# Another order inside the dense unit of a fused Fourier filter and tanh-shrink layer: second layer as 3, 3, 5, 3 calls, transform steps behind the copies out of bank X

## Chip, cores, metric

One core of one Trainium2 chip. The metric is device time of the whole program in microseconds (us).

## The reference

```python
X = np.fft.rfft(x, axis=1)                       # x: 8 x 3008 x 256, fp32
y = np.fft.irfft(X * (filt_r + 1j * filt_i), n=3008, axis=1)
h = y.reshape(24064, 256) @ w_in                 # 256 x 2048
out = (h - np.tanh(h)) @ w_out                   # 2048 x 256
```

## The kernel before

The sequences are transformed in five batches. While one batch goes through the two matrix layers, the next is transformed in between, a step at a time. Both layers use a seven-product scheme for 2 x 2 blocks: seven products q = 1 to 7 and some adds in place of eight products.

The dense work runs in 192 **units**. In unit U, `up` makes the seven first-layer products, `shrink` works on the activation of unit U-1, and `down` makes the second-layer products of unit U-2. Four units make a group; their second layer accumulates in four PSUM banks (o0 to o3), and is read out in the group's last unit (`done`). Three more banks, X, Y and Z, hold first-layer results, and one bank serves all transform steps. That makes eight banks in all. The transform's matmuls write pf (first stage), pz and pe (middle stage, before and after the filter) and pu (last stage); zs is ScalarE's copy of pz, and uv is VectorE's product of pz with the filter.

```python
        # up(U, d, e, s, t): before
        mm(X, 1, True)
        mm(Y, 2, True)
        s1 = copied("s1")                 # ACT.copy out of X
        t(0)                              # transform step, if one is due here
        d()                               # a group of second-layer products
        s()                               # activation: arctan, square
        V.tensor_add(h[:, 0, :, 0:w], Y, s1)
        e()                               # in a group's last unit: read-out
        s()                               # activation: second square; VectorE multiply
        s()                               # VectorE multiply-add
        t(1)
        mm(X, 6, False)
        mm(Z, 5, True)
        u2 = copied("u2")                 # ACT.copy out of X
        d(); s(); e()
        t(2)
        mm(X, 7, False)
        u3 = copied("u3")                 # ACT.copy out of X
        V.tensor_add(h[:, 3, :, 0:w], Z, u3)
        d(); s(); e()
        t(3)
        mm(X, 4, False)
        V.tensor_copy(h[:, 2, :, 0:w], X) # VectorE copy out of X
        s(); d(); e()
        t(4)
        mm(Z, 3, False)
        V.tensor_add(h[:, 1, :, 0:w], Z, u2)
```

`mm(bank, q, ...)` is two **calls** (two halves of the hidden dimension); a call shows up as two MATMUL instructions. Bank X is one buffer: q6 accumulates onto q1 after s1 was copied out, q7 after u2, q4 after u3, and the next unit's q1 overwrites it after the VectorE copy.

```python
        # down(U): before (cut)
        at = {1: (0, 0), 2: (0, 1), 3: (1, 0), 5: (1, 1), 6: (2, 0), 7: (2, 1), 4: (3, 0)}  # q: (bank, half)
        mm(1, 2);  yield
        if done: ACT.copy(p1, product(1)); V.tensor_add(o[:, 0, 0:w], product(2), p1)
        yield
        mm(3, 5);  yield
        if done: ACT.copy(p5, product(5)); V.tensor_add(x12, product(3), p5)
        yield
        mm(6, 7);  yield
        if done: V.tensor_add(u2, product(6), p1); V.tensor_add(p1, product(7), u2)
        yield
        mm(4);     yield
        if done: ...                      # the rest of the read-out
        yield
```

## Time and profile before

| | before |
|---|---|
| time, median of 5 | 2882.08 us (2880.47 to 2883.72) |
| TensorE busy | 95% of the span |
| next busiest, VectorE / ScalarE / GpSimd | 69% / 65% / 61% |
| TensorE time lost in and between units (my sum) | 120 us of 180 us in all |

In an unbroken run of matmuls, the next one starts a fixed time after the last (0.215 us at 256 columns). Whatever a distance between two starts has above that is time lost (a stretch of matmuls at half pace counts too), and I book it under the product that comes after it. The profile's own table of waits shows less: a matmul is drawn some 0.38 us long, so a wait below 0.16 us doesn't appear, and a wait that falls on a weight load is listed under PEld.

In the lines of the profile, PE is TensorE, PEld its weight loads, DVE is VectorE, ACT ScalarE and POOL GpSimd. A line in order of time has start, duration, engine, line of the program, operation, output and inputs, and in brackets how long the engine was idle before it and what ended that.

### The profile page before, as it was taken

What the parts mean: (1) busy time and instruction counts of PE and PEld (TensorE: products, weight loads), DVE (VectorE), ACT (ScalarE), POOL (GpSimd) and SP (SyncE); (2) the same over time, 40 slices, a digit from 0 to 9 for tenths busy, and PEclk for the clock granted to TensorE, in tenths of its full rate; (3) what the DMA queues carried; (4) which work ended last, traced back from release to release, by engine and by line L of the source; (5) the groups of instructions that cost most, each with busy time, mean ns of one, the idle gap of its engine ahead of it and who ended that gap; (6) DMA issues with size and microseconds to landing.
All of it is one profiled execution on the core that took longest, in us unless ns stands there. A gap on an engine that the chain in (4) does not pass through costs nothing.

```text
span 2879.3 us, 36469 instructions
## 1 busy us (share of the span) xinstructions
PE 2748.1 (95%) x12474; PEld 2278.9 (79%) x12474; DVE 1989.3 (69%) x2214; ACT 1872.2 (65%) x2460; POOL 1743.4 (61%) x1382
## 2 busy tenths in 40 slices
PE   5789999999999999999999999999999999999996
PEld 3467777888878787888877888888888888888885
DVE  4675666766776677766677777766777777777765
ACT  3555666666767676666666676666666676666663
POOL 4345777544677767645576777655476666555544
PEclk7889999999999999999999999999999999999998
DMA  9644443232233332222323233112233222110100
GB/s 270 180 150 116 114 110 91 62 93 81 70 76 84 76 75 53 57 81 83 87 71 75 68 78 81 36 45 67 51 75 81 53 55 56 24 28 16 26 11 16
DMA packets 328061, 217.46 MB, mean 76 GB/s; under 512 B 229085, under 2 KB 280405, under 8 KB 327674
## 3 DMA queue, kind: packets, MB, share of 16 engines
q1 hardware_dynamic: 273176, 160.50, 23.6%
q10 hardware_dynamic: 52738, 51.33, 5.9%
q0 software_dynamic: 1952, 3.22, 0.5%
q8 instruction: 100, 1.64, 0.2%
q14 instruction: 95, 0.78, 0.1%
HBM read 138.81 MB, written 79.17 MB: 76 GB/s over the span
## 4 chain that ended last, share of the span: by engine, by line
PE 69%; DVE 9%; ACT 8%; POOL 5%; issue 4%; DMA 3%; SPq 1%; ACTq 0%; DVEq 0%; POOLq 0%
PE o L590 27%; PE x L483 18%; PE z L483 8%; PE y L483 5%; PE pe L364 3%; PE pu L447 3%; DVE h L544 3%; PE pz L383 3%; ACT y L539 2%; PE pf L304 2%; ACT y L540 1%; POOL t L465 1%; ACT u L489 1%; DVE uv L398 1%; DVE h L519 1%
## 5 line engine op out<-in xcount | busy, mean ns | idle before, releaser
L590 PE MATMUL o<-t,wd 128*128 128x256 f32 (+2 forms) x3072 | 777.9, 376 | 1.8 <-POOL t L464 1.3
L544 DVE TENSOR_TENSOR h<-h,y 128x1024 f32<-128x1024 f32 (+2 forms) x384 | 589.7, 1536 | 256.1 <-ACT y L540 255.9
L462 POOL TENSOR_TENSOR t<-h 128x512 f32<-128x512 f32 (+2 forms) x192 | 240.1, 1250 | 767.5 <-DVE h L548 582.3
L590 PEld LDWEIGHTS o<-t,wd 128*128 128x128 f32 x3072 | 582.0, 191 | 74.4 <-POOL t L464 1.9
L483 PE MATMUL x<-tu,wu 128*128 128x256 f32 (+2 forms) x2304 | 592.2, 380 | 16.5 <-ACT u L489 15.5
L590 PE MATMUL o<-h,wd 128*128 128x256 f32 (+2 forms) x2304 | 581.6, 375 | 0.2 <-DVE h L548 0.2
L548 DVE SCALAR_TENSOR_TENSOR h<-sq,h 128x1024 f32<-128x1024 f32 (+2 forms) x384 | 566.6, 1476 | 20.8 <-ACT y L539 0.5
L483 PEld LDWEIGHTS x<-tu,wu 128*128 128x128 f32 x2304 | 430.2, 191 | 157.2 <-issue 73.2
L590 PEld LDWEIGHTS o<-h,wd 128*128 128x128 f32 x2304 | 431.3, 190 | 70.8 <-issue 18.5
L545 ACT ACTIVATE sq<-y,near_b 128x1024 f32<-128x1024 f32 (+2 forms) x384 | 435.4, 1134 | 5.8 <-DVE h L548 1.1
L539 ACT ACTIVATE y<-h 128x1024 f32<-128x1024 f32 (+2 forms) x384 | 400.0, 1042 | 14.8 <-ACT e L367 6.8
L489 ACT COPY s<-x 128x512 f32<-128x512 f32 (+2 forms) x192 | 110.7, 577 | 458.2 <-PE x L483 449.6
L540 ACT ACTIVATE y<-y 128x1024 f32<-128x1024 f32 (+2 forms) x384 | 399.3, 1040 | 12.2
L465 POOL TENSOR_TENSOR t<-t,h 128x512 f32<-128x512 f32 (+2 forms) x192 | 306.7, 1597 | 0.0
L489 ACT COPY u<-x 128x512 f32<-128x512 f32 (+2 forms) x384 | 219.2, 571 | 73.0 <-PE x L483 35.5
L399 POOL TENSOR_TENSOR zs<-zs,ft 128x512 f32<-128x512 f32 x112 | 166.3, 1485 | 142.3 <-ACT zs L397 142.2
L463 POOL TENSOR_TENSOR t<-h,t 128x512 f32<-128x512 f32 (+2 forms) x192 | 241.6, 1258 | 15.0
L464 POOL TENSOR_TENSOR t<-h 128x512 f32<-128x512 f32 (+2 forms) x192 | 249.5, 1300 | 0.0
L400 POOL TENSOR_TENSOR uv<-uv,zs 128x512 f32<-128x512 f32 x112 | 211.3, 1887 | 16.0 <-DVE uv L398 7.8
L483 PE MATMUL x<-ut,wu 128*128 128x256 f32 (+2 forms) x768 | 200.0, 383 | 12.2 <-DVE h L519 10.7
L483 PE MATMUL z<-tu,wu 128*128 128x256 f32 (+2 forms) x768 | 195.4, 377 | 0.5 <-DVE h L525 0.5
L483 PE MATMUL z<-ut,wu 128*128 128x256 f32 (+2 forms) x768 | 194.8, 376 | 0.0
(113 smaller groups left out, 3236.6 us busy)
## 6 DMA issues: line engine op xcount, KB each, us to landing
a<-ct SPq DMA_DIRECT2D x64, 384.0 KB
ct<-e ACTq DMA_DIRECT2D x128, 192.0 KB
ft<-filt SPq DMA_DIRECT2D x96, 256.0 KB
out_dram<-ot SPq DMA_DIRECT2D x1408, 16.0 KB
ct<-a ACTq DMA_DIRECT2D x80, 256.0 KB
x_sb<-in_x_dram SPq DMA_DIRECT2D x69, 256.0 KB
e<-ct SPq DMA_DIRECT2D x33, 512.0 KB
fg<-fg SPq DMA_DIRECT2D x40, 392.0 KB
```

Source lines behind the costliest of these rows:

```text
L462: G.tensor_sub(t[0], b[0][1], b[0][0])
L463: G.tensor_sub(t[1], b[1][1], t[0])
L464: G.tensor_sub(t[2], b[1][1], b[0][1])
L465: G.tensor_sub(t[3], t[1], b[1][0])
L483: nc.tensor.matmul(bank[:, k], wu[:, q - 1, (2 * u + k) * 128:(2 * u + k + 1) * 128], rhs[q - 1], start=(first and k == 0), stop=True, ski ...
L489: ACT.copy(t, X)
L539: ACT.activation(y[k], ht[k], AF.Arctan, scale=S)
L540: ACT.activation(y[k], y[k], AF.Square)
L544: V.tensor_mul(ht[k], ht[k], y[k])
L545: ACT.activation(sq[k], y[k], AF.Square, bias=near_b, scale=A)
L548: V.scalar_tensor_tensor(out=ht[k], in0=sq[k], scalar=K, in1=ht[k], op0=ALU.add, op1=ALU.mult)
L590: nc.tensor.matmul(product(q), wd[:, q - 1, (2 * u + k) * 128: (2 * u + k + 1) * 128], rhs[q - 1][:, k], start=(u == 0 and k == 0 and q == ...
```

## The change

The intent is the same distance, five calls, between each two products that write X, and a ScalarE and VectorE queue in which the copies out of X stand ahead of the transform's work. Core of the diff:

```diff
         mm(X, 1, True)
+        s1 = copied("s1")
         mm(Y, 2, True)
-        s1 = copied("s1")
         t(0)
 ...
+        mm(X, 6, False)
+        u2 = copied("u2")
+        mm(Z, 5, True)
         t(1)
-        mm(X, 6, False)
-        mm(Z, 5, True)
-        u2 = copied("u2")
         d(); s(); e()
-        t(2)
         mm(X, 7, False)
         u3 = copied("u3")
         V.tensor_add(h[:, 3, :, 0:w], Z, u3)
+        t(2)
         d(); s(); e()
-        t(3)
         mm(X, 4, False)
         V.tensor_copy(h[:, 2, :, 0:w], X)
+        t(3)
 ...                                   # t(4) likewise behind mm(Z, 3) and its add
-        mm(1, 2)
+        mm((1, 0), (2, 0), (1, 1))                       # (q, half)
         yield
         if done:
             ACT.copy(p1, product(1))
+        yield
+        mm((2, 1), (3, 0), (3, 1))
+        yield
+        if done:
             V.tensor_add(o[:, 0, 0:w], product(2), p1)
         yield
-        mm(3, 5)
+        mm((5, 0), (6, 0), (5, 1), (6, 1), (7, 0))
         yield
         if done:
             ACT.copy(p5, product(5))
+            V.tensor_add(u2, product(6), p1)
             V.tensor_add(x12, product(3), p5)
-        yield
-        mm(6, 7)
+            G.tensor_add(o[:, 0, w:2 * w], u2, x12)
+        yield
+        mm((7, 1), (4, 0), (4, 1))
         yield
 ...
```

More of the change, by code (lines that the diff above doesn't have):

```diff
@@ L522, in up @@
         e()
-        t(4)
         mm(Z, 3, False)
         V.tensor_add(h[:, 1, :, 0:w], Z, u2)
+        t(4)
     def shrink(U):
@@ L587, in mm @@
         def mm(*qs):
-            for k in range(2):
-                for q in qs:
-                    nc.tensor.matmul(product(q), wd[:, q - 1, (2 * u + k) * 128:
-                                                    (2 * u + k + 1) * 128],
-                                     rhs[q - 1][:, k], start=(u == 0 and k == 0 and q == qs[0]),
-                                     stop=(u == 3 and k == 1), skip_group_check=True)
+            for q, k in qs:
+                nc.tensor.matmul(product(q), wd[:, q - 1, (2 * u + k) * 128:(2 * u + k + 1) * 128],
+                                 rhs[q - 1][:, k],
+                                 start=(u == 0 and k == 0 and at[q][1] == 0),
+                                 stop=(u == 3 and k == 1), skip_group_check=True)
         done = u == 3
@@ L609, in down @@
             ACT.copy(p5, product(5))
+            V.tensor_add(u2, product(6), p1)
             V.tensor_add(x12, product(3), p5)
+            G.tensor_add(o[:, 0, w:2 * w], u2, x12)
         yield
-        mm(6, 7)
+        mm((7, 1), (4, 0), (4, 1))
         yield
         if done:
-            V.tensor_add(u2, product(6), p1)
             V.tensor_add(p1, product(7), u2)
-        yield
-        mm(4)
-        yield
-        if done:
             V.tensor_add(o[:, 1, 0:w], product(4), p1)
-            G.tensor_add(o[:, 0, w:2 * w], u2, x12)
             G.tensor_add(o[:, 1, w:2 * w], p1, p5)
```

## The prediction

> **What bounds the kernel now.** I read the page first, then the table of stretches, then who PE waited for, then the order of work inside single units. A "unit" is one of 192 rounds that computes seven first-layer products (q 1, 2, 6, 5, 7, 4, 3 into the PSUM banks X, Y, X, Z, X, X, Z), seven second-layer products in four groups (d), and up to five transform steps t(0) to t(4).
>
> ```profile
> PE 2748.1 (95%) x12474; PEld 2278.9 (79%) x12474; DVE 1989.3 (69%) x2214; ACT 1872.2 (65%) x2460; POOL 1743.4 (61%) x1382
> ```
> TensorE is busy 95% and every other engine at most 69%. The work is the same after the change, so only TensorE's idle moments can move the time.
>
> ```profile
> 121.70:537.50 415.80, 377.98 (x1556) 290.40 (x1555) 266.82 (x315) 266.96 (x363) 262.95 (x202) 0.96 0.43 113
> ...
> 1215.00:1892.00 677.00, 671.83 (x3052) 554.83 (x3052) 476.56 (x513) 458.87 (x600) 433.46 (x328) 1.00 0.29 73
> ```
> Columns are span, then PE, PEld, DVE, ACT and POOL busy time. The first 24 units leave PE idle 38 us; a later stretch of 48 units leaves 5 us. A matmul of 256 columns is shown as about 380 ns, but in an unbroken run the next starts 0.215 us after it, so short waits hide in the shown durations. I therefore summed, from the starts of single matmuls in the trace, what each start-to-start distance exceeds its usual value by (0.215 us at 256 columns). That gives about 180 us lost: 60 before the first unit, 60 in units 0 to 23, 60 in units 24 to 191. By what stood after the wait in units 24 to 191: q1 of the next unit 26 us, q4 9 us, q7 5 us, q6 under 1 us; the rest is spread thinly. These four are the products that write bank X and wait for a copy out of it.
>
> ```profile
> PE x L483 <- ACT u L489: 15.5, 12, 3.8
> PE pe L364 <- DVE uv L398: 13.5, 18, 2.6
> PE x L483 <- DVE h L519: 10.7, 26, 0.9
> ```
> The waits of PE (total us, times, longest) name the same two culprits: ScalarE's copies u and VectorE's copy h out of X. One such wait, in the timeline at 1636 to 1641 us:
>
> ```profile
> 1636.37 1.02 PE L383 MATMUL pz<-a,fg 94*128 94x512 f32 x2
> 1637.23 1.03 PE L483 MATMUL x<-tu,wu 128*128 128x256 f32 x4
> 1638.09 0.58 ACT L397 COPY zs<-pz 64x512 f32<-64x512 f32 x1
> 1639.11 0.69 DVE L398 TENSOR_TENSOR uv<-pz,ft 128x512 f32<-128x512 f32 x1 [1.03 <-ACT zs L397]
> 1639.72 0.68 DVE L519 COPY h<-x 128x512 f32<-128x512 f32 x1
> 1640.45 1.13 PE L483 MATMUL x<-ut,wu 128*128 128x256 f32 x4 [0.47 <-DVE h L519]
> ```
> q4 (1637.23) is done near 1638.3, but the copy starts at 1639.72, behind the transform's multiply uv, which itself waited for ScalarE. PE then stalls. The change aims at this.
>
> **What the Trainium skill says.** "PSUM — Partial Sum Buffer", section "Engine vs sequencer instructions": ScalarE and VectorE queues are strict FIFO, and matmuls keep program order. The lines above agree: h waits 1.4 us behind uv though its data is there. The same page, section "PSUM bank collisions raise a hardware error", has accesses of two engines to one bank kept apart; uv starting only after ScalarE's zs (1.03 us of idling) agrees. "TensorE: Matmul & The Clock Gate", section "What's actually happening": after an idle window the array runs at half clock. The trace agrees: after q4's wait of 3.8 us at 186.3 us its four matmuls take 2.08 us in place of 1.03.
>
> **The change part by part.** In units of one call (two matmuls, 0.43 us), the calls between a writer of X and the next writer of X:
> - q1 to q6: 6 before, 5 after.
> - q6 to q7: 6, then 5.
> - q7 to q4: 4, then 5.
> - q4 to next q1: 4, then 5.
>
> The amount of work is unchanged: 14 + 14 calls. The transform step t(1) moves from before q6 to between q5 and d; t(2) from before q7 to after it; t(3) from before q4 to after it and after the h copy; t(4) behind q3. On ScalarE and VectorE their copies and multiplies now queue behind the copy out of X. t(0) stays in place.
>
> Gain at q1: 26 us. VectorE's copy no longer queues behind uv of t(3). 25 units have that step at t(3); 23 of them stall, 9 us together. In the other units (15 us of waits) the copy hangs on the chain q7, copy, VectorE, copy; between q7 and the next q1 there are now 14 calls instead of 12, 0.86 us more, and t(2) as well. The waits there average about 0.6 us. I take 24 us as gone.
>
> Gain at q4: 9 us. 7 us fall in units with the step pz or pe at t(2), whose ScalarE copies (two of 0.59, or 0.58 plus 0.32 of DMA issue) stood ahead of the copy u3. Now they stand behind it, and one call more covers it. I take 8 us as gone.
>
> Loss at q7, where I differ from the intent. The copy u2 is often not released by q6: ScalarE reaches it late. Unit 28, without any stall before:
>
> ```profile
> 592.21 1.03 PE L483 MATMUL x<-ut,wu 128*128 128x256 f32 x4
> 593.27 0.58 ACT L489 COPY s<-x 128x512 f32<-128x512 f32 x1 [2.87 <-PE x L483]
> 593.93 1.02 PE L304 MATMUL pf<-x_sb,wf_sb 128*128 128x512 f32 x2
> 594.99 0.58 ACT L305 COPY a<-pf 128x512 f32<-128x512 f32 x1 [1.14 <-PE pf L304]
> 595.61 0.37 ACTq L306 DMA_DIRECT2D ct<-a  x1
> 596.02 1.06 ACT L539 ACTIVATE y<-h 128x1024 f32<-128x1024 f32 x1 [0.44 <-ACT a L305]
> 597.11 1.06 ACT L540 ACTIVATE y<-y 128x1024 f32<-128x1024 f32 x1
> 598.20 1.15 ACT L545 ACTIVATE sq<-y,near_b 128x1024 f32<-128x1024 f32 x1
> 599.25 0.57 ACT L489 COPY u<-x 128x512 f32<-128x512 f32 x1
> 599.97 1.03 PE L483 MATMUL x<-tu,wu 128*128 128x256 f32 x4
> ```
> From q1 (592.21) ScalarE runs s1, t(0)'s copy and DMA issue, three activations, then u2, which ends at 599.82. This time is set by q1 and t(0), neither of which moves. q7 starts at 599.97, after 16 calls and t(0). After the change only 14 calls lie before it: 599.97 - 2 x 0.43 = 599.1. It must wait for 599.88, so it loses about 0.78 us. Where t(2) is filled as well, its 0.86 us also leaves the time before q7. Where t(1) is filled, its matmuls stay before q7 while its ScalarE work moves behind u2, so there is enough time.
>
> I did this subtraction for units 24 to 190: slack between the end of u2 and q7 today, less 0.86 us (0.43 where u2 is not held by ScalarE), less 0.86 us if t(2) is filled, plus t(1)'s ScalarE time. By occupied steps: t(0) and t(3) alone, 12 units, slack 0.06 becomes -0.85; t(0), t(2), t(4), 15 units, 1.27 becomes -0.43 on average; no step at all, 31 units, 1.27 becomes 0.40, no wait. The sum is 38 us in 59 units, nearly all with t(0) filled and t(1) empty. A blocked product today also loses about 0.1 us at its second matmul: 6 us more. Less the 5 us lost there now, q7 costs about +39 us.
>
> Smaller: in fourth units with pz at t(1) and pu at t(2), pu needs the transform's single PSUM bank; the distance shrinks from 8 calls to 5 and zs now waits behind u2, about 0.6 us in 6 units, +4.
>
> Units 0 to 23: q4's wait of 3.8 us at 186 us comes from weight conversion on ScalarE ahead of u3; that goes behind it, up to 6 us with the half-clock time, but a wait of 4.3 us for x_sb follows and may take half of it back. Where the steps alternate pz and pe, the waits of pe fall at t(1) (7 calls of distance, not 4) and rise at the next t(0) (4, not 6). I put this whole part at -8.
>
> Sum: -24 - 8 + 39 + 4 - 8 = about +3; rounding up a little because q7's longer cycle leaves the gains at q4 and q1 partly unused: 2886.
>
> **The rivals.**
> 1. The intended gain: even spacing of 5 removes the waits at q1 and q4 and adds none, as u2 rarely binds. Then -32 - 8, 2842. For it: the two named waits of PE. Against it: u2 in unit 28 ends 0.15 us before q7 today, and 16 calls are cut to 14.
> 2. Losses at q7 plus a bank queue: transform steps come later and closer (t(1) to t(2) 8 calls to 5), so pe, pu and pf wait for the single transform bank, and the early units with a step at every place lose. Then about +25, 2907. For it: pe already waits 13.5 us for uv. Against it: later steps are mostly two or more places apart.
> 3. Early cascade: the first units lose their waits with the half-clock stretches, 15 to 20 us less, with the late part even: 2867. Against it: waits for x_sb set their own time.
>
> **Range and chances.** A gain above 2% would need 58 us, nearly all that units 24 to 191 lose in total, and a loss above 2% needs the q7 stall at over twice my count. Hence 0.02 and 0.03. The range runs from rival 3 to rival 2.
>
> **What would show it.** Right: waits of PE for the h copy near zero; waits for the u copies up to 30 to 45 us, before q7, in units with t(0) filled and t(1) empty, 0.4 to 1.0 us each; q4 with almost none; TensorE's busy count unchanged. Wrong: u2 ending well before q7 in such units (rival 1), or pe and pu waits above 35 us (rival 2).

## The result, and the profile after

The changed kernel took **2911.64 us** (median of 5, 2910.81 to 2915.46) against 2882.08: ratio 1.0109, interval 1.0095 to 1.0123. Within 2%, but 30 us longer, and above the range that I gave, which ended at 2907.

The first line of the page has the same count of matmuls, and no engine has become the bound:

```profile
PE 2756.1 (95%) x12474; PEld 2270.0 (78%) x12474; DVE 1956.2 (67%) x2214; ACT 1862.3 (64%) x2460; POOL 1765.1 (61%) x1382
```

The waits of PE after the change (total us, times, longest):

```profile
PE x L483 <- ACT u L489: 31.3, 34, 5.4
PE o L590 <- DVE pu L614: 15.7, 23, 1.5
...
PE pe L364 <- DVE uv L398: 8.7, 11, 1.4
...
PE o L590 <- ACT p L603: 7.5, 14, 0.7
...
PE x L483 <- DVE h L519: 1.9, 6, 0.7
```

The wait for the VectorE copy h is nearly gone (10.7 before), the one for the ScalarE copies u has doubled (15.5 before): both as predicted. But two lines are new, and I had not thought of either: second-layer matmuls (L590) wait for `DVE pu L614`, the add that reads product 6, and for `ACT p L603`, the copy of product 1. For this one add, the view by line tells who waited for it:

```profile
L614 DVE TENSOR_TENSOR pu<-o,p x48: 350/417/425, 218.1 to 2885.3; 128x256 f32<-128x256 f32 x43, 128x192 f32<-128x192 f32 x3, 128x224 f32<-128x224 f32 x2
...
who waited for it (us, times):
  PEld o L590: 31.2, 37
  PE o L590: 15.7, 23
```

Before the change, where this add is L615, no matmul waited for it, and six weight loads did, 1.6 us in all. One such wait in the order of time:

```profile
1707.31 1.03 PE L483 MATMUL x<-tu,wu 128*128 128x256 f32 x4
1707.72 1.22 DVE L545 TENSOR_TENSOR h<-h,y 128x1024 f32<-128x1024 f32 x1
1708.04 0.36 ACT L613 COPY p<-o 128x256 f32<-128x256 f32 x1
1708.85 0.42 DVE L614 TENSOR_TENSOR pu<-o,p 128x256 f32<-128x256 f32 x1
...
1709.33 0.92 PE L590 MATMUL o<-t,wd 128*128 128x256 f32 x3 [0.99 <-DVE pu L614]
```

At 1707.31 q4's matmuls start; 0.86 us later, at 1708.17, product 7's second half could follow. It follows at 1709.33. The add L614 reads product 6 out of bank o2, product 7's second half writes to the other half of the same bank, and the program keeps the two apart. The add is late because VectorE first finishes a 1.22 us multiply.

The wait that I did foresee, in unit 28, the unit of the prediction:

```profile
582.15 1.03 PE L483 MATMUL x<-ut,wu 128*128 128x256 f32 x4
583.22 0.59 ACT L489 COPY s<-x 128x512 f32<-128x512 f32 x1 [2.43 <-PE x L483]
584.94 0.59 ACT L305 COPY a<-pf 128x512 f32<-128x512 f32 x1 [1.14 <-PE pf L304]
585.56 0.37 ACTq L306 DMA_DIRECT2D ct<-a  x1
585.97 1.06 ACT L540 ACTIVATE y<-h 128x1024 f32<-128x1024 f32 x1 [0.44 <-ACT a L305]
587.06 1.06 ACT L541 ACTIVATE y<-y 128x1024 f32<-128x1024 f32 x1
588.15 1.15 ACT L546 ACTIVATE sq<-y,near_b 128x1024 f32<-128x1024 f32 x1
589.20 0.57 ACT L489 COPY u<-x 128x512 f32<-128x512 f32 x1
589.91 1.10 PE L483 MATMUL x<-tu,wu 128*128 128x256 f32 x4 [0.69 <-ACT u L489]
```

ScalarE runs as before, q7 comes two calls earlier and waits. From start to start it loses 0.86 us (the 0.69 in brackets counts from the drawn end of the matmul before); predicted was 0.78.

Lost time by the product that waited, in us, over all 192 units, from one profiled run of each kernel:

| kernel | time against before | lost in all | q1 | q4 | q7 | products 2 and 7 |
|---|---|---|---|---|---|---|
| before | 1 | 180 | 27 | 19 | 12 | 4 |
| after | 1.0109 | 210 | 6 | 6 | 50 | 37 |
| e1 other banks | 1.005 | 189 | 6 | 6 | 61 | 3 |
| e2 steps alone | 0.9972 | 173 | 27 | 9 | 17 | 5 |
| e3 spacing alone | 1.0116 | 206 | 5 | 18 | 27 | 37 |
| e4 square behind u2 | 1.0049 | 194 | 11 | 10 | 10 | 44 |
| e5 banks + square | 0.9922 | 156 | 13 | 14 | 11 | 3 |
| e6 spacing + banks | 1.0019 | 183 | 6 | 21 | 36 | 3 |
| e7 readers late | 1.0037 | 193 | 8 | 6 | 60 | 3 |
| e8 4, 3, 4, 3 | 0.9967 | 167 | 18 | 23 | 10 | 3 |

### The profile page after: what moved, and what is told of

The parts are those of the page before. It is cut to its first block, busy times and chain, and to the rows that moved or that the text cites. A ratio compares the mean times of both kernels' runs of the same rounds, so it can differ in the third digit from the quotient of the medians.

```text
span 2909.8 us, 36555 instructions
## 1 busy us (share of the span) xinstructions
PE 2756.1 (95%) x12474; PEld 2270.0 (78%) x12474; DVE 1956.2 (67%) x2214; ACT 1862.3 (64%) x2460; POOL 1765.1 (61%) x1382
## 4 chain that ended last, share of the span: by engine, by line
PE 71%; ACT 14%; DVE 5%; issue 4%; DMA 3%; POOL 1%; ACTq 1%; DVEq 0%; SPq 0%; POOLq 0%
PE o L590 29%; PE x L483 17%; PE z L483 8%; PE y L483 5%; ACT y L540 4%; PE pe L364 3%; PE pu L447 3%; ACT y L541 3%; PE pz L383 3%; PE pf L304 2%; ACT u L489 2%; DVE h L545 2%; ACT zs L396 1%; ACT zs L397 1%; ACT sq L546 1%
## 5 line engine op out<-in xcount | busy, mean ns | idle before, releaser
L545 DVE TENSOR_TENSOR h<-h,y 128x1024 f32<-128x1024 f32 (+2 forms) x384 | 541.7, 1411 | 333.2 <-ACT y L541 333.0
L590 PE MATMUL o<-t,wd 128*128 128x256 f32 (+2 forms) x3072 | 719.2, 377 | 17.7 <-DVE pu L614 15.7
L590 PEld LDWEIGHTS o<-t,wd 128*128 128x128 f32 x3072 | 573.9, 191 | 144.6 <-issue 43.1
L549 DVE SCALAR_TENSOR_TENSOR h<-sq,h 128x1024 f32<-128x1024 f32 (+2 forms) x384 | 585.1, 1524 | 20.8 <-ACT u L489 0.9
L590 PE MATMUL o<-h,wd 128*128 128x256 f32 (+2 forms) x2304 | 552.4, 376 | 7.5 <-ACT p L603 7.5
L590 PEld LDWEIGHTS o<-h,wd 128*128 128x128 f32 x2304 | 428.4, 190 | 112.7 <-issue 46.8
L513 DVE TENSOR_TENSOR h<-z,u 128x512 f32<-128x512 f32 (+2 forms) x192 | 130.6, 680 | 221.3 <-ACT u L489 220.9
L500 DVE TENSOR_TENSOR h<-y,s 128x512 f32<-128x512 f32 (+2 forms) x192 | 129.9, 677 | 123.4 <-PE y L483 108.0
L400 POOL TENSOR_TENSOR uv<-uv,zs 128x512 f32<-128x512 f32 x112 | 204.8, 1828 | 8.9
```

The costliest lines, as they stand in the source:

```text
L545: V.tensor_mul(ht[k], ht[k], y[k])
L549: V.scalar_tensor_tensor(out=ht[k], in0=sq[k], scalar=K, in1=ht[k], op0=ALU.add, op1=ALU.mult)
L590: nc.tensor.matmul(product(q), wd[:, q - 1, (2 * u + k) * 128:(2 * u + k + 1) * 128], rhs[q - 1][:, k], start=(u == 0 and k == 0 and at[q] ...
```

## The experiments

All eight gave correct results. My theory after the result: the change pays at q1 and q4, and loses in two places, at q7 (as predicted) and in each group's last unit, where finished products are now read between two matmuls of their bank. The rivals: the engines are simply late there; or one half of the change is good and the other bad.

### e1: products dealt to banks so that no read falls inside a bank's run

```diff
-        at = {1: (0, 0), 2: (0, 1), 3: (1, 0), 5: (1, 1), 6: (2, 0), 7: (2, 1), 4: (3, 0)}
+        at = {1: (0, 0), 2: (1, 0), 3: (1, 1), 5: (2, 0), 6: (2, 1), 7: (3, 0), 4: (3, 1)}
```

> The changed kernel with the seven second-layer products dealt out to the four PSUM banks in another way (1 alone; 2 and 3; 5 and 6; 7 and 4), so that no finished product is read from a bank while another product of the same bank still has matmuls to come. Order, readers and transform steps stay. Theory A (in each fourth unit the copy of product 1 and the add on product 6 now fall between two matmuls of their bank, which makes TensorE wait): the waits ahead of product 7's and product 2's matmuls, 25 + 11 us, go, and the time is 2911 - 33 = about 2878 us, with q7's waits a little up (49 to about 53), since those waits covered some of them. Rival B (VectorE and ScalarE are simply late there, and whatever comes next on TensorE inherits the delay): the time stays within 8 us of 2911, and the lost time shows up at q4, q7 or the next unit's q1.

Measured: 2893.20 us against 2879.26, ratio 1.005. The waits at products 2 and 7 are gone, 37 to 3 us, and no PE wait for `DVE pu` or `ACT p` is left among the waits:

```profile
PE x L483 <- ACT u L489: 41.2, 47, 5.5
```

Cause confirmed, size half of what I expected (17 us, taking the two ratios' difference, not 33). q7 took 10 us back. In the units with t(0) filled and t(1) empty, the 12 that are also a group's last unit lost 2.8 us at q7 after the change, and 12.7 us here: the wait at product 2 stands just before q7 and had covered it. Rival B has a part of the truth.

### e2 and e3: one half of the change each

e2 is the kernel before with the unit's body of the changed one. e3 is the kernel before with the second layer of the changed one.

```diff
 # e2, e3: each takes one of the two halves of the diff shown above
```

> The kernel before with the transform steps moved as in the change, but the second layer left at 4, 4, 4, 2. Theory A (the moved steps are the good half: they take the waits at q1 and q4 away, and the loss at q7 comes from the two calls taken out between q1 and q7): q1 27 to about 5 us, q4 19 to about 5, q7 12 to 18, no waits at products 2 and 7; about 2882 - 32 = 2850 us. Rival B (moving the steps is what makes u2 late for q7): q7's waits reach 40 us or more and the time is 2890 or more.

> The kernel before with the second layer as 3, 3, 5, 3 as in the change, but the transform steps left where they were. Theory A: the waits at products 2 and 7 in each fourth unit appear in full (30 to 36 us), q7 waits about 25 us (t(2) still stands before it and covers it), q1 falls to about 12 and q4 to about 12 us; about 2918 us (2905 to 2930). Rival B (the even spacing is good and the moved steps do the harm): 2882 or less.

Measured: e2 2872.08 us (ratio 0.9972), e3 2911.47 us (1.0116), before 2879.26. e3 is as Theory A had it: the waits at products 2 and 7 come with the split alone, 37 us, whatever the steps do; only q1 and q4, 5 and 18 us, are not the 12 and 12 that I expected. e2 gained 8 us, not 32. The table tells why. Summed over the kernel, **q4 hangs on the steps** (19 to 9 in e2, 18 in e3) and **q1 on the spacing** (27 in e2, 5 in e3). I had expected the moved steps to free q1 too. In sum they don't: in e2 PE still waits for the VectorE copy.

```profile
PE x L483 <- DVE h L518: 13.0, 28, 1.6
PE x L483 <- ACT u L489: 12.1, 6, 4.6
```

Sorted by units, the trace of e2 shows that the steps do act where I expected it, and that waits come up elsewhere. In the 25 units whose predecessor has pz at t(3), q1 lost 9.3 us before and 0.9 in e2; in all other units it rose, from 16 to 21 us in units 24 to 191 and from 1 to 5 us in the first 24. Of q4's 19 us, 10 lay in the first 24 units and are gone in e2. In the 25 later units with pz or pe at t(2), q4 lost 6.8 us before, 7.9 in e3 and nothing in e2; but later units with t(1) filled lost 4.8 us there in e2, against 1.0 before.

So the good half isn't the steps alone: q1's gain needs the fifth call, and the fifth call was taken from in front of q7.

### e4: the third activation behind u2

```diff
         e()
+        mm(X, 6, False)
+        u2 = copied("u2")
         s()
         s()
-        mm(X, 6, False)
-        u2 = copied("u2")
```

> The changed kernel with the third activation of the block (and its two VectorE operations) issued behind the copy u2 instead of ahead of it, nothing else. Theory A (q7 waits because u2 sits at the end of ScalarE's run q1, s1, t(0)'s copy, three activations, u2): u2 is ready 1.15 us earlier, q7's waits fall from 49 to about 10 us, the waits at products 2 and 7 stay or rise a little, about 2911 - 38 = 2873 us. Rival B (u2 is late for another reason, as a wait for VectorE or for q6 itself): q7's waits stay above 35 us and the time within 10 us of 2911.

Measured: 2894.79 us, ratio 1.0049. q7's lost time fell from 50 to 10 us, as Theory A had it: u2 is late because of ScalarE's own queue. The time fell by only 17 us, not 38. Products 2 and 7 rose from 37 to 44, q1 and q4 from 11 to 21:

```profile
PE o L590 <- DVE pu L614: 19.6, 25, 1.7
PE x L483 <- ACT u L489: 12.2, 10, 4.3
```

### e5: both repairs

The edits of e1 and e4 together. It was run on another chip.

> The changed kernel with both repairs: the other dealing of products to banks (e1) and the third activation behind u2 (e4). If the two losses are separate causes, the waits at products 2 and 7 (44 us in e4) and at q7 (61 us in e1) are both gone: 17 us from e4, and about 38 us more, so 25 us under the kernel before, about 2856 us. If each only hid behind the other and a third wait takes over (q4, q1, the transform's bank), it stays above 2875 us.

Measured: 2857.68 us against 2880.97, ratio 0.9922 (0.9905 to 0.9938), where 2856 was expected. Each repair alone gave 0.6%, both give 1.9% against the changed kernel. The two losses are separate causes, and each hid a part of the other. With both gone, the waits for the copies out of X are small:

```profile
PE x L483 <- ACT u L489: 14.7, 18, 4.3
PE x L483 <- DVE h L519: 5.3, 13, 1.3
```

This is the fastest version: 23 us under the kernel before, still within 2%.

### e6: even spacing without the reads inside a bank

e3 with the banks of e1. It was run on another chip.

> The kernel before with 3, 3, 5, 3 and the other dealing to banks, transform steps where they were: the even spacing alone, without reads in the middle of a bank. q1 stays near 5 us as in e3, products 2 and 7 wait for nobody, q7 rises from 27 to about 35 us since it loses their cover. 2911 - 37 + 8: about 2883 us, the kernel before within 8 us. If the spacing by itself is worth its gain at q1 (22 us), 2862 or less.

Measured: 2884.55 us against 2880.97, ratio 1.0019. Even spacing in itself, with the steps where they were, is worth nothing here: 21 us less at q1, 24 us more at q7.

### e7: banks as they were, readers later

```diff
         mm((1, 0), (2, 0), (1, 1))
         yield
+        yield
+        mm((2, 1), (3, 0), (3, 1))
+        yield
         if done:
             ACT.copy(p1, product(1))
-        yield
-        mm((2, 1), (3, 0), (3, 1))
-        yield
-        if done:
             V.tensor_add(o[:, 0, 0:w], product(2), p1)
 ...                        # the add on product 6 likewise behind mm((7, 1), (4, 0), (4, 1))
```

> The changed kernel, banks as they were, but in the fourth unit the copy of product 1 moved behind product 2's last matmul and the add on product 6 behind product 7's last matmul. If the reads between two matmuls of one bank are the cause, this gives what e1 gave: no waits at products 2 and 7, q7 about 58 us, about 2893 us (within 6). If e1 gained by its other layout of the banks, this one stays at 2905 or more.

It was run on another chip. Measured: 2891.84 us, ratio 1.0037, products 2 and 7 at 3 us, q7 at 60. The same as e1 by another way: it is the read between two matmuls of one bank, not the layout.

### e8: 4, 3, 4, 3

e5 with the second layer cut into 4, 3, 4, 3 calls, 1 and 2 together in bank o0, 3 and 5 in o1, 6 alone, 7 and 4 in o3.

> An attempt at the best: steps as moved by the change, the third activation behind u2, second layer as 4, 3, 4, 3 with banks dealt out so that no product is read before its bank's last matmul (6 alone, 7 with 4). Spacing 6, 5, 4, 5 calls instead of 5, 5, 5, 5. Expected: q7 about 6, q1 about 12, q4 about 14 us; about 2854 us. If q4 needs its fifth call, 2865 or more, and e5 is the better one.

Measured: 2870.94 us against 2880.97, ratio 0.9967. q7 stays low (10 us), but q4 loses 23 us and q1 18, against 14 and 13 in e5. I missed by 17 us: q4 does need its fifth call once q7 no longer waits. Why q1 loses more than in e5, at the same distance of five calls, is not shown.

## Why the prediction was wrong

Its steps, with lost time from the trace after the change:

- **What bounds the kernel, and where it loses time**: right. Only idle moments of TensorE moved the time (lost time +30 us, time +30 us).
- **Gain at q1**, 24 us: measured 22 us in units 24 to 191. I had put 9 us of it down to uv and the rest to the two further calls. The calls alone have nearly all of it (e3, about 4 us left of 26). The steps alone free the units with uv ahead of the copy, as I had it, and lose most of that in other units (e2, 22 us left).
- **Gain at q4**, 8 us: measured 5 us there. The reason, the steps, holds: the units with pz or pe at t(2) lost 6.8 us before and nothing after the change, as in e2 and unlike e3. What is missing came up anew in units with t(1) filled, 1.0 us before and 3.5 after.
- **Loss at q7**, 39 us: measured 30 us in units 24 to 191, and 40 us in e1, where nothing covers it. By kind of unit: of the 45 units with t(0) filled and t(1) empty outside the groups' last ones, 44 stalled, 30 us together; the 20 with both filled lost 0.1 us. The cause held in e4. (A slip in my working: a slack of 0.06 less 0.86 is -0.80, not -0.85, 0.6 us over the 12 units.)
- **pu for the transform's bank**, +4: measured +3. **Units 0 to 23**, -8: measured about -8.5, in part by luck. q4 gained 8 us there, more than I had, but q7 lost the same 8 again; what remained is less waiting of pe (5 us) and of pf (2.5 us).
- **"The amount of work is unchanged: 14 + 14 calls." This is the step that failed.** It is true of the calls, but I took the new cut of the second layer as a matter of spacing alone. Products 2 and 7 are now split over two groups, and I didn't ask who reads their banks between the two. Products 1 and 2 share bank o0, 6 and 7 share o2. Before, both were complete before the first read. Now, in 48 of 192 units, the copy of product 1 and the add on product 6 come between two matmuls of one bank. That is 34 us more of lost time that the sum hadn't at all. With it the sum is +3 + 34 = +37, less the 10 us that it covers at q7: +27, where +30 was measured.

The right rival would have been a fourth. Rival 2 came nearest in size, 2907, by another cause: the waits of pe, which it would have had grow, fell from 25 to 18 us.

Left open: why q1's waits in e2 rise in the units in which no uv stood ahead of the copy, so that their sum stays at 27 us. I have not followed each.

## What to carry to other kernels

When a group of matmuls is cut differently, write down for every PSUM bank its writers and readers in the new order. A finished product that is read while its bank-mate still has matmuls to come turns a free read into a wait of TensorE. And a distance between two writers of a bank is only as good as the queue of the engine in between: count that engine's work from the event that starts it, not from the writer. Here calls were taken from the one gap that ScalarE's queue needed. Two losses can also cover one another, so repair them together before judging either.

## What the Trainium skill lacked or had wrong

- "PSUM — Partial Sum Buffer", section "PSUM bank collisions raise a hardware error", says to guard by bank and quadrant, not by address. The program does so, and the trace shows product 7's matmul waiting for a read of the other half of its bank. What the page lacks is the price: 37 us over 48 such units in the changed kernel; net of what it covered, 17 us by e1 and 21 us by e7.
- The same page, section "Summary: rules for kernel authors", says to "Evacuate promptly", for want of room, and in another row to target a different bank when reading while a matmul runs. It doesn't say which comes first. Here reading a product as soon as it was complete, with its bank still in use, cost those 17 to 21 us, and reading it later (e7) was faster.
- No page that I read tells that a blocked product loses time twice: after a wait at its first matmul, the second starts another 0.1 us late (0.86 and then 0.08 us at q7 in unit 28).
- "TensorE: Matmul & The Clock Gate", section "What's actually happening", gives idle windows of about 3.4 us ahead of half clock. In the kernel before, a wait of 2.38 us at 239 us was followed by eight matmuls at half pace, and one of 2.75 us at 507 us by none (both counted from start to start; the profile's own brackets have 2.22 and 2.59). The page calls the window free-running, so waits of one length may end differently; but both are shorter than a whole window, and no run here tells why the first was enough.
